# The order of a copy and a matmul product in the value pair of a fused attention and SwiGLU kernel

## The chip, the cores and the metric

The kernel runs on one core of a Trainium2 chip. The core has a matrix engine (TensorE, PE in the profile, with its weight loads as PEld), VectorE (DVE), ScalarE (ACT), GpSimd (POOL) and SyncE (SP, which here only issues transfers). Each engine works through its own instructions in order and waits on semaphores for the others. The metric is the device time of one execution in microseconds.

## What is computed

The reference is an attention with keys and values projected from 1024 to 64 rows, followed by a gated feed-forward block (cut, with the softmax and the joining of the heads written as calls):

```python
# batch 8, heads 8, seq 1024, head_dim 64, k_proj 64; d_model 512, d_ff 1536
k_proj = np.einsum('ks,bhsd->bhkd', E, k)
v_proj = np.einsum('ks,bhsd->bhkd', F, v)
scores = scale * np.matmul(q, k_proj.transpose(0, 1, 3, 2))
attn = softmax(scores)
x = heads_together(np.matmul(attn, v_proj))     # 8192 x 512
g = x @ w_gate
silu = g * (1.0 / (1.0 + np.exp(-g)))
val = x @ w_val
out = silu * val @ w_out                        # 8192 x 512, float32
```

Most of the arithmetic is in the three products of the feed-forward block. The change is in the second, `val = x @ w_val`.

## The kernel before, in words

**Tiling.** The 8192 rows are cut into 16 chunks c of 512 rows (two per batch). For a chunk the attention leaves `xT`: 128 partitions by 4 blocks of the contraction by 512 rows, in bfloat16. The 1536 columns of the two first weights are 12 feature blocks f of 128. The main loop runs over t = 12c + f. For each t it records the gate block (`f_g`: four matmuls of 512 columns at L530 into the PSUM tile `gps`, then ScalarE's activation, L547 or L554), one slot of attention work for a later batch, the value block (`f_v`: four matmuls at L530 into the PSUM tile `vps`, then VectorE's multiplication with the activated gate into `hT`, L648), and the "late" work: sums and products of the output stage for the chunk before (`f_m`, matmuls at L732 into `yps`, with VectorE's addition at L761) and sums that prepare products to come. The order is written out by hand: each engine executes in the order in which the code records its instructions, and the framework adds the semaphore waits that the data need.

**The value pair.** In the 13 chunks c = 2 to 14 the feature blocks 10 and 11 are not computed as two value blocks but as a pair, by a scheme of seven products in place of eight (as in Strassen's method), with the contraction, the features and the rows each cut in two. A product m (`p_mm`, L602) is two matmuls of 256 columns. Products 3 and 4 multiply plain weight blocks by differences of row blocks (`xsa`, `xsb`, made at L593 by GpSimd when c is even, by VectorE when c is odd, several blocks earlier); product 1 multiplies a sum of weights by a sum of rows.

`f_v_pair` is recorded in two parts. The first, at f = 10, takes a PSUM tile `xp` (named `vps`, two halves of 256 columns, one bank), puts product 3 in its first half and product 4 in its second, and forms on VectorE, in the SBUF tile `vt`: a copy of product 3 (L618), plus product 4 (L620). It takes a second PSUM tile `zp` (also `vps`) for product 1 and forms the next partial sum (L623). The second part, at f = 11, adds products 5 and 2 onto the halves of `xp`, subtracts these from both partial sums (L630), multiplies the two inner quarters into `hT` (L631), adds products 6 and 7 onto `zp`, and finishes the outer quarters (L636, L638). Of the tiles named `vps` there are two in turn: feature block 8 and `xp` use one, feature block 9 and `zp` the other. So the first matmul into `zp` must follow the multiplication that read feature block 9.

**Around it.** Between the two parts TensorE has the late work of f = 10 (12 matmuls at L732) and the gate block of f = 11. On VectorE the instructions around the copy are, in even chunks before the last pair (c = 14), the multiplication L648 of block 9, a sum and a reciprocal of the softmax (L402, L403), the copy, L620, L623, L761; in odd chunks L648 and a difference (L593) come before the copy, in c = 14 L648 alone. GpSimd meanwhile multiplies softmax rows (L417), adds up a check sum (`zsum`, L433) and forms sums for the output stage (L715). A second path of the program (`general`), taken only when the check sum is too large, makes no pairs.

Of the kernel before, what the change touches and what calls it, by code (L numbers as in the profile page):

```python
# [44 lines left out]
def kernel(  # L45
# [115 lines left out]
    def bank(where, shape, dt, name):  # L161
        if where == "a" and ring["wide"]:
            where = "aaz"[ring["n"] % 3]
            ring["n"] += 1
        pool, tag = banks[where]
        return pool.tile(shape, dt, name=name, tag=tag)
# [428 lines left out]
    def p_mm(c, m, ps, start=False):  # L595

        x = xT[divmod(c, CH)]
        f = [slice(i * P, (i + 1) * P) for i in PAIR]
        w = {3: wv[:, 0:2, f[0]], 4: wv[:, 2:4, f[1]]}[m] if m in (3, 4) else sums["w", m]
        xs = {2: x[:, 0:2, 0:HT], 5: x[:, 2:4, HT:CW]}[m] if m in (2, 5) else sums["x", m]  # L600
        for kt in range(2):
            nc.tensor.matmul(  # L602
                out=ps,
                lhsT=w[:, kt],
                rhs=xs[:, kt],
                start=(start and kt == 0),
                stop=(kt == 1),
                skip_group_check=True,
            )

    def f_v_pair(c, f):

        tensor_tensor = nc.vector.tensor_tensor
        if f == PAIR[0]:
            xp = gp["x"] = bank("v", [P, 2, HT], FP32, "vps")
            t = gp["t"] = fw.tile([P, 2, HT], FP32, name="vt", tag="s1", bufs=1)
            p_mm(c, 3, xp[:, 0], start=True)
            nc.vector.tensor_copy(out=t[:, 0], in_=xp[:, 0])  # L618
            p_mm(c, 4, xp[:, 1])
            tensor_tensor(out=t[:, 0], in0=t[:, 0], in1=xp[:, 1], op=ALU.add)  # L620
            zp = gp["z"] = bank("v", [P, 2, HT], FP32, "vps")
            p_mm(c, 1, zp[:, 0], start=True)
            tensor_tensor(out=t[:, 1], in0=t[:, 0], in1=zp[:, 0], op=ALU.add)  # L623
            return
        th, xp, zp, t = (gp.pop(i) for i in "pxzt")
        th = th[:].rearrange("p i t -> p (i t)")
        h = hT[c][:, PAIR[0] : PAIR[1] + 1, :].rearrange("p i t -> p (i t)")
        p_mm(c, 5, xp[:, 0])
        p_mm(c, 2, xp[:, 1])
        tensor_tensor(out=t[:], in0=t[:], in1=xp[:], op=ALU.subtract)  # L630
        tensor_tensor(  # L631
            out=h[:, HT : 3 * HT], in0=th[:, HT : 3 * HT], in1=xp[:].rearrange("p i t -> p (i t)"), op=ALU.mult
        )
        p_mm(c, 6, zp[:, 1])
        p_mm(c, 7, zp[:, 0])
        tensor_tensor(out=t[:], in0=t[:], in1=zp[:], op=ALU.add)  # L636
        h, th = (a.rearrange("p (i t) -> p i t", i=4)[:, 0::3] for a in (h, th))
        tensor_tensor(out=h, in0=th, in1=t[:], op=ALU.mult)  # L638

    def f_v(c, f, i=None):  # L640
        if paired(c, f):
            return f_v_pair(c, f)
        ps = f_mm(c, f, 1, i)
        g, th = gp.pop(0)
        if f == 0:
            hT[c] = h_pool.tile([P, NFT, CW], BF16, name="hT", tag="hT")
        if g is None:
            nc.vector.tensor_tensor(out=hT[c][:, f, :], in0=th[:], in1=ps[:], op=ALU.mult)  # L648
            return
        s1 = fw.tile([P, CW], FP32, name="s1", tag="s1", bufs=1)  # L650
        nc.vector.scalar_tensor_tensor(
            out=s1[:], in0=th[:], scalar=1.0, in1=g[:], op0=ALU.add, op1=ALU.mult
        )
        nc.vector.scalar_tensor_tensor(
            out=hT[c][:, f, :], in0=s1[:], scalar=0.5, in1=ps[:], op0=ALU.mult, op1=ALU.mult
        )
# [258 lines left out]
    with tc.manual_schedule():  # L915
# [175 lines left out]
        for t in range(NIT):  # L1091
            c, f = divmod(t, NFT)
# [42 lines left out]
```

## Time and profile before

| What | Value |
|---|---|
| Median of 3 runs | 555.32 us (555.25 to 555.66) |
| The profiled execution | 555.38 us |
| Its span in the profile | 553.8 us |
| VectorE busy | 369.4 us, 67% |
| GpSimd busy | 356.3 us, 64% |
| ScalarE busy | 262.0 us, 47% |
| L530 into `gps` / into `vps` | 772 / 672 matmuls, 196.6 / 170.9 us |
| L618 copy, L620, L623 | 13 each; medians 425, 422 and 422 ns |
| L602 | 182 matmuls and as many weight loads; matmul medians 272 to 273 ns |

The span runs from the first to the last instruction of the program; the execution takes a little longer. A matmul's duration includes the time in which its result drains, which overlaps the next matmul: the sum of durations is larger than the busy time, and the pace of TensorE is read from the distance of starts. "Idle before" in a timeline is the time since the engine's last modelled end, and the name behind the arrow is the instruction whose semaphore came last before the start.

### The profile page before, as it was taken

Reading aid. Unit: us, or ns where it says so; the run is one execution under the profiler, and the core shown is the slowest. Engines: PE = TensorE matmul, PEld = TensorE weight load, DVE = VectorE, ACT = ScalarE, POOL = GpSimd, SP = SyncE. Lnnn points to the kernel's source line nnn. Section 1 sums busy time; section 2 is a strip of 40 time slices with the busy share of each in tenths; the row PEclk is TensorE's granted clock in tenths of the full one; section 3 lists DMA queues with packets and bytes.
Section 4 is the critical chain, followed back from the end, with each engine's and each line's share of the span. In section 5 each row is a group of like instructions: output and inputs, shape, how many; then the busy total and the mean of one; then the engine's idle time right before and its main releaser. Section 6 shows DMA issues by size and latency. Waiting matters only on the chain.

```text
span 553.8 us, 9681 instructions
## 1 busy us (share of the span) xinstructions
PE 537.7 (97%) x3636; PEld 320.8 (58%) x3636; DVE 369.4 (67%) x640; ACT 262.0 (47%) x441; POOL 356.3 (64%) x456
## 2 busy tenths in 40 slices
PE   7999999999999999999999999999999999999996
PEld 4654445565556655566565665566555565556565
DVE  3787886677567765668576585666855777555553
ACT  3565454663446624546436454455444653443331
POOL 6862498577567765586665866668656766464262
PEclk9999999999999999999999999999999999999999
DMA  9999979829921798109941199304991122110113
GB/s 199 190 196 189 176 145 181 162 76 162 192 67 40 132 206 156 39 2 179 195 121 39 24 187 198 88 38 60 203 195 39 40 77 76 40 39 0 39 39 118
DMA packets 112227, 62.92 MB, mean 114 GB/s; under 512 B 65968, under 2 KB 103856, under 8 KB 112176
## 3 DMA queue, kind: packets, MB, share of 16 engines
q0 software_dynamic: 43952, 29.49, 37.7%
q1 hardware_dynamic: 67392, 31.46, 25.0%
q10 hardware_dynamic: 832, 1.31, 0.7%
q8 instruction: 29, 0.48, 0.4%
q14 instruction: 22, 0.18, 0.1%
HBM read 60.29 MB, written 16.78 MB: 139 GB/s over the span
## 4 chain that ended last, share of the span: by engine, by line
PE 87%; ACT 4%; POOL 3%; DMA 2%; DVE 2%; issue 2%; ACTq 0%; POOLq 0%; DVEq 0%
PE gps L530 27%; PE vps L530 24%; PE yps L732 23%; PE vps L602 4%; DMA wv<-in_moe_w_val_dram 2%; PE sc L372 2%; PE kvp L181 2%; PE yps L666 2%; ACT L554 1%; PE pv L476 1%; ACT ee L380 1%; POOL AAd L417 1%; DVE hT L648 1%; POOL hs L715 1%; ACT th L554 1%
## 5 line engine op out<-in xcount | busy, mean ns | idle before, releaser
L530 PE MATMUL gps<-xT,wg 128*128 128x512 bf16 (+1 forms) x772 | 196.6, 377 | 0.0
L530 PE MATMUL vps<-xT,wv 128*128 128x512 bf16 (+1 forms) x672 | 170.9, 377 | 0.7 <-DMA wv<-in_moe_w_val_dram 0.7
L715 POOL TENSOR_TENSOR hs<-hT 128x256 bf16<-128x256 bf16 x180 | 120.7, 695 | 53.6 <-DVE hT L648 30.6
L554 ACT ACTIVATE th<-gps 128x512 f32<-128x512 f32 x130 | 77.6, 597 | 151.3 <-PE gps L530 142.1
L648 DVE TENSOR_TENSOR hT<-th,vps 128x512 bf16<-128x512 f32 x130 | 88.6, 681 | 80.4 <-PE vps L530 66.5
L530 PEld LDWEIGHTS <-wv 128*128 128x128 bf16 x672 | 64.4, 98 | 77.6 <-issue 3.8
L732 PEld LDWEIGHTS <-hs 128*128 128x128 bf16 x900 | 88.0, 98 | 29.1 <-issue 0.6
L530 PEld LDWEIGHTS <-wg 128*128 128x128 bf16 x776 | 74.0, 98 | 51.6 <-issue 0.5
L417 POOL TENSOR_TENSOR AAd<-ee,zr 128x512 bf16<-128x512 f32 x56 | 58.3, 1041 | 35.9 <-DVE zr L403 28.9
L762 POOL TENSOR_TENSOR tt<-tt,ysb 128x512 f32<-128x512 f32 x28 | 35.6, 1272 | 66.2 <-DVE tt L761 66.2
L732 PE MATMUL yps<-ws,hs 128*128 128x256 bf16 x540 | 68.6, 273 | 0.2 <-DVE ysb L801 0.2
L715 DVE TENSOR_TENSOR hs<-hT 128x1536 bf16<-128x1536 bf16 (+1 forms) x49 | 60.1, 1231 | 0.1
L402 DVE TENSOR_REDUCE zr<-ee 128x8 f32<-128x512 f32 x64 | 43.4, 678 | 18.7 <-ACT ee L380 18.7
L732 PE MATMUL yps<-ws,hT 128*128 128x256 bf16 x360 | 48.8, 273 | 0.0
L732 PE MATMUL yps<-wo,hs 128*128 128x256 bf16 x360 | 48.6, 273 | 0.1
L732 PEld LDWEIGHTS <-hT 128*128 128x128 bf16 x360 | 35.2, 98 | 16.1
L593 POOL TENSOR_TENSOR xsa<-xT 128x512 bf16<-128x512 bf16 (+1 forms) x21 | 40.4, 1950 | 0.0
L380 ACT ACTIVATE ee<-sc 128x512 f32<-128x512 f32 x64 | 35.7, 607 | 4.3 <-PE sc L372 2.9
L751 POOL TENSOR_TENSOR tt<-xs 128x256 f32<-128x256 f32 x30 | 22.7, 758 | 22.3 <-ACT xs L749 22.3
L547 ACT ACTIVATE thp<-gps 128x512 f32<-128x512 f32 x26 | 15.5, 598 | 31.7 <-PE gps L530 31.7
L756 ACT COPY ysb<-yps 128x512 f32<-128x512 f32 x30 | 17.6, 585 | 27.3 <-PE yps L732 27.3
L749 ACT COPY xs<-yps 128x512 f32<-128x512 f32 x30 | 17.7, 590 | 25.1 <-PE yps L732 25.0
(131 smaller groups left out, 577.7 us busy)
## 6 DMA issues: line engine op xcount, KB each, us to landing
out_dram<-ysb SPq DMA_DIRECT2D x27, 512.0 KB, 3.0
qb<-in_q_dram POOLq DMA_DIRECT2D x14, 512.0 KB, 17.1
kb<-in_k_dram POOLq DMA_DIRECT2D x7, 1024.0 KB, 11.8
vb<-in_v_dram POOLq DMA_DIRECT2D x7, 1024.0 KB, 14.1
wo<-in_moe_w_out_dram POOLq DMA_DIRECT2D x2, 768.0 KB, 21.9
out_dram<-ysb SPq DMA_DIRECT2D x6, 256.0 KB, 2.4
kraw<-in_k_dram ACTq DMA_DIRECT2D x2, 512.0 KB, 4.9
qb<-in_q_dram POOLq DMA_DIRECT2D x4, 256.0 KB, 7.9
```

The lines of the kernel that those rows point to most:

```text
L380: nc.scalar.activation(out=e[:].rearrange("p h j k -> p (h j k)"), in_=ps[:].rearrange("p a k -> p (a k)"), func=AF.Exp, scale=scale,)
L402: nc.vector.reduce_sum(out=z, in_=e[:], axis=AX.X)
L417: eng.tensor_tensor(out=a.rearrange("p j h k -> p h j k"), in0=ee.pop((b, u))[:], in1=r.unsqueeze(3).to_broadcast([P, 4, 2, KP]), op=ALU.mult,
L530: nc.tensor.matmul(out=ps[:, ts], lhsT=(wg, wv)[w][:, kt, f * P : (f + 1) * P], rhs=x[:, kt, ts], start=(kt == 0), stop=(kt == NKT - 1),)
L554: nc.scalar.activation(out=th[:], in_=ps[:], func=AF.Silu)
L593: eng.tensor_tensor(out=sums["x", m], in0=i0, in1=i1, op=op)
L602: nc.tensor.matmul(out=ps, lhsT=w[:, kt], rhs=xs[:, kt], start=(start and kt == 0), stop=(kt == 1), skip_group_check=True,)
L648: nc.vector.tensor_tensor(out=hT[c][:, f, :], in0=th[:], in1=ps[:], op=ALU.mult)
L715: eng.tensor_tensor(out=hs[c, m][:, fs, :], in0=quarter(hT[c], *a)[:, fs], in1=quarter(hT[c], *b)[:, fs], op=op,)
L732: nc.tensor.matmul(out=ps, lhsT=lhsT, rhs=ws[m][:, f, :] if rhs is None else rhs, start=(start and f == 0), stop=(f == HF - 1), skip_group ...
L751: nc.gpsimd.tensor_tensor(out=t[:, 0], in0=xs[:, 0], in1=xs[:, 1], op=ALU.add)
L762: nc.gpsimd.tensor_tensor(out=t[:], in0=t[:], in1=yo[c, p][:, 1:3], op=ALU.subtract)
```

## The change

In the first part of the value pair two statements change places: the code records product 4's matmuls ahead of VectorE's copy of product 3.

```diff
             p_mm(c, 3, xp[:, 0], start=True)
+            p_mm(c, 4, xp[:, 1])
             nc.vector.tensor_copy(out=t[:, 0], in_=xp[:, 0])
-            p_mm(c, 4, xp[:, 1])
             tensor_tensor(out=t[:, 0], in0=t[:, 0], in1=xp[:, 1], op=ALU.add)
             zp = gp["z"] = bank("v", [P, 2, HT], FP32, "vps")
             p_mm(c, 1, zp[:, 0], start=True)
```

The copy is L618 before and L619 after. As the two are on different engines, the order of the instructions on each engine stays as it was; what differs is which instruction waits for which. The values computed are the same.

## The prediction

> **What bounds the kernel now.** I read the page first, then who TensorE waited for, then the timeline around the edited lines.
>
> ```profile
> span 553.8 us, 9681 instructions
> PE 537.7 (97%) x3636; PEld 320.8 (58%) x3636; DVE 369.4 (67%) x640; ACT 262.0 (47%) x441; POOL 356.3 (64%) x456
> PEclk9999999999999999999999999999999999999999
> ```
>
> TensorE (PE) is busy 97% of the span at an undiminished clock, and no other engine passes 67%. So the time is the sum of what TensorE issues and of the moments in which it can't issue. The next view lists those moments: what waited, for whom, microseconds in total, times, longest. Of its eight rows these are the three largest.
>
> ```profile
> PE vps L602 <- DVE vt L618: 4.3, 8, 0.6
> PE vps L602 <- POOL zsum L433: 2.9, 5, 0.6
> PE warm L954 <- DVE zeros L932: 1.4, 1, 1.4
> ```
>
> L602 is the matmul of the value pair. It was held 8 + 5 = 13 times, once in each of the 13 paired chunks; together 7.2 us. The other six rows (1.4 and five under 1 us) are single events of the start and the tail. So in the steady part TensorE has one kind of stall, and it is in the edited lines. In an even chunk (c = 4) it looks like this; columns are start, duration, engine, line, what, and the idle time with its releaser.
>
> ```profile
> 176.25 0.65 DVE L648 TENSOR_TENSOR hT<-th,vps 128x512 bf16<-128x512 f32 x1
> 177.12 0.38 PE L602 MATMUL vps<-xsa,wv 128*128 128x256 bf16 x2
> 177.53 0.20 DVE L403 RECIPROCAL zr<-zr 128x8 f32<-128x8 f32 x1
> 177.65 0.37 DVE L618 COPY vt<-vps 128x256 f32<-128x256 f32 x1
> 177.83 0.22 POOL L433 TENSOR_TENSOR zsum<-zsum,zr 128x16 f32<-128x16 f32 x1
> 178.08 0.39 PE L602 MATMUL vps<-xsb,wv 128*128 128x256 bf16 x2 [0.58 <-POOL zsum L433]
> 178.31 0.38 PE L602 MATMUL vps<-xsa,xsb 128*128 128x256 bf16 x2
> 178.51 0.42 DVE L620 TENSOR_TENSOR vt<-vt,vps 128x256 f32<-128x256 f32 x1 [0.49 <-PE vps L602]
> 178.53 1.47 PE L732 MATMUL yps<-ws,hs 128*128 128x256 bf16 x12
> 179.03 0.42 DVE L623 TENSOR_TENSOR vt<-vt,vps 128x256 f32<-128x256 f32 x1
> 180.11 0.42 DVE L761 TENSOR_TENSOR tt<-tt,yps 128x256 f32<-128x256 f32 x1 [0.65 <-PE yps L732]
> 180.70 0.60 PE L602 MATMUL vps<-xT,xsb 128*128 128x256 bf16 x4
> 181.14 0.27 PE L602 MATMUL vps<-xsa,xsb 128*128 128x256 bf16 x1
> ```
>
> Product 3 is issued at 177.12, VectorE copies its result from 177.65 to 178.02, and product 4 starts at 178.08, 0.06 us behind the copy's end. Product 4 writes the other half of the PSUM tile that the copy reads, and the listing of the program's instructions has its first weight load wait for the copy. In an odd chunk (c = 3) TensorE shows the same step:
>
> ```profile
> 143.12 0.39 PE L602 MATMUL vps<-xsa,wv 128*128 128x256 bf16 x2
> 144.03 0.38 PE L602 MATMUL vps<-xsb,wv 128*128 128x256 bf16 x2 [0.52 <-DVE vt L618]
> ```
>
> **The stall's price.** One 256-column matmul is issued every (1.47 - 0.27) / 11 = 0.109 us: the row of 12 at 178.53 takes 1.47, and one alone lasts 0.27. Two take 0.22. So c = 4 loses 178.08 - 177.12 - 0.22 = 0.74 us, and c = 3 loses 144.03 - 143.12 - 0.22 = 0.69. The waits view shows less (0.58 and 0.52) because it counts from the modelled end of the last matmul, which comes 0.273 - 0.109 = 0.164 us after the next could have been issued. Over all: 7.2 + 13 x 0.164 = 9.3 us.
>
> **The change part by part.** Nothing is added and every engine keeps its order; the listings of both programs differ in waits alone.
>
> 1. *Removed: product 4's wait for the copy.* It keeps a wait for its input difference: on GpSimd in even chunks (L593 at 165.30 for 1.16 us in c = 4, over 10 us early) and on VectorE in odd ones (the view of L593 has the first of these at 141.8 for 0.42, in c = 3, 0.9 us ahead of product 3). Neither holds it. So product 4 is issued right behind product 3: -9.3 us.
>
> 2. *Added: a wait in front of product 1.* It writes the pair's second tile, whose last reader is the multiplication of feature block 9 (L648). Earlier that was covered by the wait for the copy. In c = 4 that L648 ends at 176.90, before product 3 starts, while product 1 would now be issued at 177.12 + 4 x 0.109 = 177.56. It is met 0.66 us early and I take its cost as 0. From below: a met wait may be free, and the spacing around the old wait may even tighten by 0.01 a chunk, 0.1 in all. From above: if the hand-over can't overlap, it costs the 0.06 us seen from copy end to product 4 and a 0.10 us weight load, 0.16 x 13 = 2.0 us. No row shows a met wait at this place. The nearest are products 5 and 2 at 180.70: product 5 and, from 181.14, product 6 carry met waits for L620 and L623 in the listing, and the four matmuls between take 0.44, 0.110 each. So I take 0.
>
> 3. *Moved: the copy.* It now waits for product 4. In c = 4 that product would be issued at 177.34 and 177.45, and done at 177.45 + 0.27 = 177.72; VectorE comes free of L403 at 177.73. With the 0.04 us that the copy took to start after its product in c = 3 (143.12 + 0.39 = 143.51, start 143.55), the copy runs from 177.76 at the odd chunks' 0.43 us to 178.19. In even chunks it is thus not delayed by more than 0.1 us, because VectorE was behind anyway; in odd ones it starts 0.22 us later.
>
> 4. *Queued behind the copy on VectorE:* L620, L623, then L761 and the rest. L620 no longer waits for TensorE. With the 0.10 us between L620's end (178.93) and L623's start, L620 runs 178.29 to 178.71 and L623 178.81 to 179.23. What is late next? L761 is released by TensorE, and its 180.11 becomes 180.11 - 0.74 = 179.37: VectorE is free 0.14 us before. Product 5 (180.70, now 179.96) overwrites what L620 reads: 1.25 us to spare. So the copy's 0.43 us is hidden by what TensorE issues between products 4 and 5: product 1, the 12 matmuls of L732 and the four of the next gate block. If that cover were gone, product 5 would wait up to 0.43 + 0.10 us a chunk, 6.9 us in all.
>
> The Trainium skill, page "VectorE: DVE Perf Modes", section "The DRAIN you can't avoid", speaks against item 4: after each VectorE operation it puts a flush of its duration less 266 ns, 0.16 us here, where the row has 0.10. By that page the estimate has L623 end 0.11 us later, still 0.03 before L761 is released, so the sum would be the same by both.
>
> Sum: -9.3 + 0 + 0. The profiled execution took 555.38 us, 1.55 more than its span; the median of the runs is 555.32. So the span goes to 544.5 and the time to 555.3 - 9.3 = **546.0 us**. TensorE's stages are all released by TensorE's own earlier work, so that a shift early on stays: where VectorE waited for TensorE (L620, L761 above) it waits still.
>
> **The rivals.**
>
> *A. In five even chunks GpSimd is the releaser.* The waits view says so: POOL zsum L433, five times. That sum runs 177.83 to 178.05, just before product 4. If it were so, five chunks would keep 0.74 us each, 3.7 us: 549.7 us. Against it: product 4's GpSimd wait in the listing is for L593 of the block differences, long done; the copy ends within 0.03 us of the sum by accident of this stage. 4%.
>
> *B. The wait only moves.* If product 1 had to wait for the copy itself, it would start at 178.19 + 0.06 = 178.25 instead of 178.31 in even chunks (0.06 won), and in odd ones at 144.24 instead of 144.25. That is 6 x 0.06 + 7 x 0.01 = 0.4 us: 554.9 us. For it: the copy still stands between the products in VectorE's queue and TensorE's wait is counted in VectorE's operations. Against: the count in the listing is that of L648, and product 1 writes another tile. 4%.
>
> *C. Slower: VectorE's chain becomes late at product 5.* One mechanism: L620 now stands behind a later copy, and product 5 waits for it. It costs from the point where L620 ends 1.25 us later than I have it, and it eats the whole gain at 1.25 + 0.72 = 1.97 us. At 2.1 us late the loss is 13 x 0.13 = 1.7: 557.0 us. For it: in even chunks VectorE has no idle time between L648 and the copy. Against: it would take four more operations of 0.42 + 0.10 us in that queue, and the order has none. 3%.
>
> **How the numbers follow.** My forecast has 88%, A 4%, B 4%, C 3%, and 1% is left for what I don't see. Range of the forecast: from 545.5 (the 0.1 of item 2 and the runs' spread of 0.4) to 548.0 (the 2.0 of item 2). As it holds 88%, it need not reach to A. A measurement here can tell about 0.2%, 1.1 us. Faster: forecast and A, 92%. Within: B and the rest, 5%. Slower: C, 3%.
>
> **What would show it.** Right: the waits view has no row of L602 for L618 or L433; products 3, 4 and 1 stand 0.22 us apart; TensorE is busy 537.7 - 13 x 0.164 = 535.6 us (the tails now overlap) of a span near 544.5, 98%. Item 3: the copy starts about 0.04 us after product 4 or right behind L403. Item 4: L620 has no idle time for TensorE before it, L761 still has some. Wrong: a row L602 for L648 or L619 (B), a gap ahead of the four matmuls of L602 near 180 (C), or a PEclk below 9, which would be a cause outside this list.

## The result and the profile after

| | before | after |
|---|---|---|
| Median of 6 runs | 555.40 us (555.05 to 555.66) | 546.95 us (546.61 to 547.50) |
| The profiled execution | 555.38 us | 547.50 us |
| Its span | 553.8 us | 545.8 us |

The ratio is 0.9849, with a 95% interval of 0.9836 to 0.9861: 8.45 us less, where 9.3 were forecast. The head of the page after:

```profile
span 545.8 us, 9668 instructions
PE 535.5 (98%) x3636; PEld 321.5 (59%) x3636; DVE 369.6 (68%) x640; ACT 262.2 (48%) x441; POOL 356.2 (65%) x456
PEclk9999999999999999999999999999999999999999
```

The clock is the same, and TensorE's busy time fell by 2.2 us. Of this, 430.69 - 429.12 = 1.57 lie behind the first product 3 (c = 2): the 13 matmul tails of 0.164, which now overlap the next matmul, less the 0.09 at seven places that is told below. The other 0.6 lie in front of it, where the two programs are the same. The 13 instructions that are gone are waits: L620 had two and has one. The view of what TensorE waited for, four largest of nine rows:

```profile
PE warm L954 <- DVE zeros L932: 1.4, 1, 1.4
PE vps L530 <- DMA wv<-in_moe_w_val_dram: 0.9, 1, 0.9
PE sc L372 <- DVE BD L169: 0.7, 1, 0.7
PE efp L942 <- DMA Eraw<-in_E_dram: 0.7, 1, 0.7
```

L602 is gone from it, for L618 and for L433. What is left are single events of the start and the tail. The timeline of the even chunk c = 4:

```profile
175.66 0.65 DVE L648 TENSOR_TENSOR hT<-th,vps 128x512 bf16<-128x512 f32 x1
...
176.52 0.38 PE L602 MATMUL vps<-xsa,wv 128*128 128x256 bf16 x2
...
176.74 0.38 PE L602 MATMUL vps<-xsb,wv 128*128 128x256 bf16 x2
...
176.94 0.20 DVE L403 RECIPROCAL zr<-zr 128x8 f32<-128x8 f32 x1
176.96 0.38 PE L602 MATMUL vps<-xsa,xsb 128*128 128x256 bf16 x2
...
177.16 0.42 DVE L619 COPY vt<-vps 128x256 f32<-128x256 f32 x1
177.18 1.47 PE L732 MATMUL yps<-ws,hs 128*128 128x256 bf16 x12
177.24 0.22 POOL L433 TENSOR_TENSOR zsum<-zsum,zr 128x16 f32<-128x16 f32 x1
...
177.62 0.42 DVE L620 TENSOR_TENSOR vt<-vt,vps 128x256 f32<-128x256 f32 x1
178.14 0.42 DVE L623 TENSOR_TENSOR vt<-vt,vps 128x256 f32<-128x256 f32 x1
...
178.76 0.42 DVE L761 TENSOR_TENSOR tt<-tt,yps 128x256 f32<-128x256 f32 x1 [0.19 <-POOL hs L715]
...
179.35 0.60 PE L602 MATMUL vps<-xT,xsb 128*128 128x256 bf16 x4
```

Products 3, 4 and 1 and the first of L732 stand 0.22 us apart, the pace of two matmuls. Product 1's new wait, for L648, was met 0.65 us before it started. GpSimd's sum starts 0.5 us after product 4, so product 4 does not need it. VectorE's chain ends at 178.56, 0.2 ahead of L761. L761 stands 1.58 us behind the first of L732, as it did before (178.53 to 180.11): it is still TensorE that it waits for, although the row names GpSimd. In c = 14 the same 0.19 is put down to L732.

In the odd chunk c = 3 one distance is off. ScalarE's row is the four casts out of the attention's PSUM tiles (L485), which it makes in a row.

```profile
143.23 2.05 ACT L485 CAST xT<-pv 128x512 bf16<-128x512 f32 x4
143.34 0.38 PE L602 MATMUL vps<-xsb,wv 128*128 128x256 bf16 x2
...
143.56 0.38 PE L602 MATMUL vps<-xsa,xsb 128*128 128x256 bf16 x2
...
143.87 1.47 PE L732 MATMUL yps<-ws,hs 128*128 128x256 bf16 x12
```

From product 1 to L732 it is 0.31 us, not 0.22. The first matmul of L732 takes the PSUM bank that the first of these casts empties; a cast's median is 0.598 us, so that cast ends at 143.23 + 0.60 = 143.83, and the matmul starts 0.04 behind it. In the same chunk before, the casts stood where they stand now:

```profile
143.24 2.05 ACT L485 CAST xT<-pv 128x512 bf16<-128x512 f32 x4
...
144.46 1.47 PE L732 MATMUL yps<-ws,hs 128*128 128x256 bf16 x12
```

L732 came 144.46 - 143.84 = 0.62 us behind the cast. The change would bring it 0.69 us nearer, and it needs the 0.04 behind the cast's end. By these rounded rows 0.11 us has to be given back (0.69 + 0.04 - 0.62); the distance shows 0.09 (0.31 - 0.22). It is so in each of the six odd chunks, and in c = 2, where the distance is the same 0.31: 0.6 us in all.

### The profile page after: what moved, and what is told of

Same layout as the page of the kernel before. It is cut to its first block, busy times and chain, and to the rows that moved or that the text cites. A ratio compares the mean times of both kernels' runs of the same rounds, so it can differ in the third digit from the quotient of the medians.

```text
span 545.8 us, 9668 instructions
## 1 busy us (share of the span) xinstructions
PE 535.5 (98%) x3636; PEld 321.5 (59%) x3636; DVE 369.6 (68%) x640; ACT 262.2 (48%) x441; POOL 356.2 (65%) x456
## 4 chain that ended last, share of the span: by engine, by line
PE 88%; DMA 8%; POOL 2%; issue 0%; ACT 0%; DVE 0%; POOLq 0%; DVEq 0%; ACTq 0%
PE gps L530 28%; PE yps L732 25%; PE vps L530 24%; PE vps L602 4%; DMA qTd<-qb 3%; PE sc L372 2%; DMA qb<-in_q_dram 2%; PE kvp L181 2%; DMA Fraw<-in_F_dram 1%; PE pv L476 1%; PE yps L666 1%; DMA wv<-in_moe_w_val_dram 1%; POOL wv L144 0%; POOL AA L417 0%; POOL wg L144 0%
## 5 line engine op out<-in xcount | busy, mean ns | idle before, releaser
L554 ACT ACTIVATE th<-gps 128x512 f32<-128x512 f32 x130 | 77.6, 597 | 151.2 <-PE gps L530 140.2
L648 DVE TENSOR_TENSOR hT<-th,vps 128x512 bf16<-128x512 f32 x130 | 88.6, 681 | 81.0 <-PE vps L530 67.1
L732 PEld LDWEIGHTS <-hs 128*128 128x128 bf16 x900 | 88.0, 98 | 29.7 <-issue 0.6
L732 PE MATMUL yps<-ws,hs 128*128 128x256 bf16 x540 | 68.6, 272 | 0.2 <-DVE ysb L801 0.2
L732 PE MATMUL yps<-ws,hT 128*128 128x256 bf16 x360 | 48.8, 273 | 0.0
L732 PE MATMUL yps<-wo,hs 128*128 128x256 bf16 x360 | 48.6, 273 | 0.1
L732 PEld LDWEIGHTS <-hT 128*128 128x128 bf16 x360 | 35.2, 98 | 16.0
L551 ACT ACTIVATE th<-gps 128x512 f32<-128x512 f32 x35 | 20.9, 598 | 16.7 <-PE gps L530 15.4
```

Of the source, the lines that this page charges most:

```text
L554: nc.scalar.activation(out=th[:], in_=ps[:], func=AF.Silu)
L732: nc.tensor.matmul(out=ps, lhsT=lhsT, rhs=ws[m][:, f, :] if rhs is None else rhs, start=(start and f == 0), stop=(f == HF - 1), skip_group ...
```

## The experiments

All times are medians, beside the kernel before on the same chip (555.47 us in the first four, 555.52 in the others); a ratio is to that kernel, with its 95% interval in brackets. Each diff is against the changed kernel.

**The exchange in the even chunks alone.**

```diff
-            p_mm(c, 4, xp[:, 1])
+            if c % 2 == 0:
+                p_mm(c, 4, xp[:, 1])
             nc.vector.tensor_copy(out=t[:, 0], in_=xp[:, 0])
+            if c % 2 != 0:
+                p_mm(c, 4, xp[:, 1])
```

> The exchange is made in the seven even chunks alone (c = 2, 4, ... 14); the odd ones keep the copy between the products. My theory: product 4's wait in even chunks is for the copy, although the waits view named GpSimd's zsum in five of them. The stalls read from the timeline of before are 0.80 (c = 2), 5 x 0.74 and 0.68, less the 0.09 that c = 2 gives back at L732 in the profile of after: 5.1 us off 555.4, so 550.3 us (549.9 to 550.8), and no row of L602 for L433. Rival A (GpSimd is the releaser in five even chunks): only c = 2 and c = 14 gain, 1.4 us, so 554.0 us, and the five waits for L433 stay.

550.06 us, ratio 0.990 [0.9885, 0.9915]. The largest row of TensorE's waits:

```profile
PE vps L602 <- DVE vt L620: 3.1, 6, 0.5
```

L620 is the copy's line in this kernel. The six odd stalls are left, and none is named for GpSimd. A gain of 5.4 us fits the stalls read for seven even chunks (5.1), not the 1.4 of rival A. What the waits view named in those five was an event that came just before the start, not the one waited for.

**The exchange in the odd chunks alone**: the same edit with the parity turned.

> The exchange is made in the six odd chunks alone. My theory: the stalls of 0.68 go, and 0.09 comes back in each as the distance from product 1 to the first matmul of L732 (0.20 in place of 0.11), where that matmul now waits for ScalarE's cast of a PSUM bank (L485). 6 x 0.59 = 3.5 us off 555.4: 551.9 us (551.4 to 552.3); with even_only the two gains sum to that of the whole change. Rival (nothing is given back inside the chunks, and what the change lacks against the forecast lies in the start of the program alone): 6 x 0.68 = 4.1 us, 551.3 us.

551.79 us, ratio 0.9933 [0.9919, 0.9946]: 3.7 us. This lies between 3.5 and 4.1, too near to both to decide by the medians. TensorE's timeline of c = 3 decides:

```profile
143.34 0.38 PE L602 MATMUL vps<-xsa,xsb 128*128 128x256 bf16 x2
143.65 1.47 PE L735 MATMUL yps<-ws,hs 128*128 128x256 bf16 x12
```

It is 0.31 again (L735 is L732 here). The two halves sum to 5.4 + 3.7 = 9.1 us, beside 8.45 and 8.7 us in two measurements of the whole change; the runs of one kernel spread over 0.3 to 1.2 us, so this is a sum within what can be told. The table of starts, further on, allows a closer sum.

**Product 1 between the copy and product 4.**

```diff
             p_mm(c, 3, xp[:, 0], start=True)
-            p_mm(c, 4, xp[:, 1])
             nc.vector.tensor_copy(out=t[:, 0], in_=xp[:, 0])
-            tensor_tensor(out=t[:, 0], in0=t[:, 0], in1=xp[:, 1], op=ALU.add)
             zp = gp["z"] = bank("v", [P, 2, HT], FP32, "vps")
             p_mm(c, 1, zp[:, 0], start=True)
+            p_mm(c, 4, xp[:, 1])
+            tensor_tensor(out=t[:, 0], in0=t[:, 0], in1=xp[:, 1], op=ALU.add)
```

> The copy stays right behind product 3, but product 1 (which writes the other PSUM tile) is issued before product 4 (which writes the tile that the copy reads). My theory: product 4 alone waits for the copy and starts at the same distance from product 3 as before, while product 1's 0.22 us is now spent inside the wait: 13 x 0.22 = 2.8 us off 555.4, 552.6 us (552.0 to 553.2), and the waits view keeps 13 rows of L602 for the copy, each 0.22 shorter. Rival (any product behind the copy waits for it, whatever tile it writes): 555.4 us. Second rival (it is enough that the next product is of another tile; the stall goes whole): 547 us.

552.73 us, ratio 0.9949 [0.9936, 0.9963]: 2.7 us. The timeline of c = 4:

```profile
176.51 0.38 PE L602 MATMUL vps<-xsa,wv 128*128 128x256 bf16 x2
...
176.73 0.38 PE L602 MATMUL vps<-xsa,xsb 128*128 128x256 bf16 x2
...
177.05 0.37 DVE L618 COPY vt<-vps 128x256 f32<-128x256 f32 x1
...
177.48 0.39 PE L602 MATMUL vps<-xsb,wv 128*128 128x256 bf16 x2 [0.36 <-POOL zsum L433]
```

Product 1, of the other tile, goes at TensorE's own pace. Product 4 starts 0.97 us behind product 3, as before (0.96), and 0.06 behind the copy's end. The waits view again puts five of the 13 waits down to GpSimd's sum, where I expected all at the copy; the two rows together fell from 7.2 to 4.3 us, 0.22 a chunk. So the stall was the wait for the copy out of product 4's own tile, and it can be filled with whatever writes elsewhere. Both rivals fall.

**Another bank for the attention's fourth product.** The change, and:

```diff
-        put(s0 + 44, u_PVt, b, 0, (0, 1), ("aa", "yz"))
+        put(s0 + 44, u_PVt, b, 0, (0, 1), ("aa", "yg"))
```

> The change as it is, and in the odd chunks the attention's fourth product takes a PSUM bank of the gate ring in place of the bank that the first matmul of L732 writes behind product 1. My theory: in the odd chunks that matmul waited for ScalarE's cast out of that bank; the distance from product 1's second matmul to it falls from 0.20 to 0.11 us in six chunks, 0.54 us in all: 546.4 us (546.0 to 546.8) beside 546.95 for the change alone; c = 2 keeps its 0.20. Rival (the 0.09 is a cost of the weight load or of VectorE's reading beside TensorE, not of that bank): the distance stays 0.20 and the time 546.95.

546.01 us (545.93 to 546.53), ratio 0.9831 [0.9817, 0.9844]. The timeline of c = 3:

```profile
142.41 2.05 ACT L485 CAST xT<-pv 128x512 bf16<-128x512 f32 x4
...
142.74 0.38 PE L602 MATMUL vps<-xsa,xsb 128*128 128x256 bf16 x2
...
142.96 1.47 PE L732 MATMUL yps<-ws,hs 128*128 128x256 bf16 x12
```

The distance is 0.22, with the casts as late against TensorE as they were. So the 0.09 was the wait for that bank. In c = 2, which this edit doesn't touch, the distance stays 0.31, as expected. From product 3 of c = 2 to the end of the span it is 544.5 - 110.97 = 433.5 us, beside 545.8 - 111.78 = 434.0 for the change alone: the 0.5 us expected. This version has the lowest median of all; of the 0.94 us by which it lies below 546.95, only these 0.5 are shown to come from the bank.

**Two kernels again, for their starts.**

> The kernel before, unchanged, for a second profile of its start. My theory: what the change lacks against the forecast beyond the 0.6 us given back at L732 is the start of the program, which differs from run to run with its transfers: product 3 of c = 2 began at 111.06 us in the profile of before and at 111.79 in that of after, though both programs are the same up to there. It should begin anywhere between 110.8 and 111.9 here, with the time within 555.0 to 555.8. Rival (the change itself makes the start later): here within 0.1 of 111.06 again.

> The changed kernel, unchanged, for a second profile of its start. My theory: product 3 of c = 2 begins between 110.8 and 111.9 us and not at 111.79 again; the distance from there to the end of the span is 434.0 within 0.1 as in the first profile; time 546.6 to 547.2. Rival (the change itself makes the start later): within 0.1 of 111.79 again.

The same program gave 555.33 and 546.79 us (ratio to before 0.9842 [0.9828, 0.9855] for the latter). The start of product 3 of c = 2, up to which all of these are the same program:

| profile | product 3 of c = 2, us | span - that |
|---|---|---|
| before | 111.06 | 442.7 |
| before, again | 110.98 | 442.8 |
| after | 111.78 | 434.0 |
| after, again | 111.35 | 434.1 |
| after, other bank | 110.97 | 433.5 |
| after, two more copies | 111.07 | 434.2 |
| after, five more copies | 110.89 | 445.1 |
| exchange in even chunks | 110.96 | 437.5 |
| exchange in odd chunks | 110.83 | 439.3 |
| product 1 between | 110.90 | 439.8 |

The two profiles of the changed kernel differ by 0.43, and they are the latest of the ten. Two profiles of before agree within 0.1, which by itself is what the rival said; that five other versions with the exchange, three of them with it in all chunks, start at 110.83 to 111.07 speaks against it. Behind the start the change is worth 442.7 - 434.0 = 8.7 us. The halves, reckoned so before rounding, are worth 5.23 and 3.55, in sum 8.78. Here the odd half fits 3.5 (0.09 given back in each chunk) and not the rival's 4.1.

**Two, then five more copies on VectorE.** In the changed kernel, behind the copy:

```diff
+            for _ in range(2):
+                nc.vector.tensor_copy(out=t[:, 1], in_=xp[:, 0])
```

They write a half of `vt` that is overwritten before it is read.

> The changed kernel with two more copies of product 3 on VectorE behind the first, into the half of vt that L623 overwrites later: they add about 0.45 to 0.53 us each to the chain between product 4 and product 5. My theory: the cover between products 4 and 5 is 1.2 us a chunk (1.25 in the forecast), so that 0.9 to 1.06 us of it is hidden: 546.9 to 547.8 us, no row of L602 for VectorE in the waits view above 0.3 us in all. Rival C's reading (VectorE's chain stands close behind TensorE there): product 5 waits in each chunk, 13 x 0.5 to 1.0 us: 553 us or more.

546.86 us, ratio 0.9844 [0.9828, 0.9859]: 26 more VectorE instructions cost nothing that can be measured. In c = 3 the addition starts 1.13 us behind the first copy in place of 0.46, so the two moved it by 0.67, less than I expected and about half of the cover.

> The same with five more copies: 2.25 to 2.65 us more on VectorE's chain. My theory: the cover of 1.2 us is used up, and product 5 waits for L620, or product 6 for L623, by 1.0 to 1.4 us in each of the 13 chunks: 560 to 566 us. If the time stays below 550, the cover is larger than I read it; if it is above 575, it was not there at all.

557.53 us, ratio 1.004 [1.0025, 1.0056]: below the range that I gave. The view of TensorE's waits has one large row, and the timeline of c = 3 shows it (L622 is L620 here):

```profile
PE vps L602 <- DVE vt L622: 7.4, 13, 0.6
```

```profile
144.02 0.42 DVE L619 COPY vt<-vps 128x256 f32<-128x256 f32 x1 [1.52 <-PE vps L602]
...
144.37 2.25 DVE L621 COPY vt<-vps 128x256 f32<-128x256 f32 x5
...
145.44 1.03 PE L530 MATMUL gps<-xT,wg 128*128 128x512 bf16 x4
...
146.53 0.41 DVE L622 TENSOR_TENSOR vt<-vt,vps 128x256 f32<-128x256 f32 x1
147.00 0.60 PE L602 MATMUL vps<-xT,xsb 128*128 128x256 bf16 x4 [0.53 <-DVE vt L622]
...
147.05 0.42 DVE L625 TENSOR_TENSOR vt<-vt,vps 128x256 f32<-128x256 f32 x1
...
147.52 0.60 PE L602 MATMUL vps<-xsa,xsb 128*128 128x256 bf16 x4
```

Five copies moved the addition from 0.46 behind the first copy's start (143.76 and 144.22 in after) to 2.51: 2.05 us, 0.41 each and not 0.45 or more. Product 5 stalls for 0.53 + 0.164 = 0.7 us, so 2.05 - 0.7 = 1.35 was hidden. In c = 4 product 5 stands 3.61 us behind product 3 in place of 2.83, so 2.05 - 0.78 = 1.27 was hidden there. Over all the waits come to 7.4 + 13 x 0.164 = 9.5 of the 10.7 us. Most of the rest is product 6: it writes the tile that L625 (L623 in the other kernels) reads, starts 0.05 behind L625's end (147.47), and stands 0.52 us behind product 5, where it is 0.44 in after (179.35 and 179.79 in c = 4): 13 x 0.08 = 1.0. The place and the kind of the wait are as expected; I had over-sized what a copy adds.

## Why the prediction was right, and where it was short

**Item 1, product 4's wait (9.3 us): right.** Products 3 and 4 now stand 0.22 us apart, and the even and odd halves of the change gave 5.4 and 3.7 us where the stalls read from the timeline were 5.2 and 4.1. The sign that I gave, a busy time of 535.6 us, was met (535.5) partly by luck: behind the first product 3 the busy time fell by 1.57 and not by 2.1, and the start of the program, which the change doesn't touch, supplied the rest.

**Item 2, product 1's new wait (0, at most 2.0): right at its lower end.** It is met 0.65 us early (forecast 0.66), and the distance to product 1 is 0.22.

**Item 3, the copy's new place: right.** It starts at 177.16, 0.04 behind product 4's end (177.12) and just after VectorE comes free of L403 (177.14), 0.64 us behind product 3's start as forecast (177.76 - 177.12). In c = 14, where VectorE is idle before it, it is 0.64 too.

**Item 4, the chain behind it: right in VectorE, and short on ScalarE.** VectorE's cover of 1.25 us between products 4 and 5 was shown to be there: two more copies are hidden, five are not, and the hidden part is 1.27 in c = 4, for which it was forecast, and 1.35 in c = 3. The step that was off is the sum, "-9.3 + 0 + 0". Under "what is late next" I followed VectorE's queue and product 5, and counted the 12 matmuls of L732 as cover without asking what releases them. Their first waits for ScalarE's cast, which stays where it was while TensorE comes 0.69 us earlier; 0.62 us of distance was there. The term that I put at 0 measured 7 x 0.09 = 0.6 us, and a bank that isn't shared takes it to 0 in six of the seven chunks. "TensorE's stages are all released by TensorE's own earlier work" was too broad: the casts too follow TensorE's matmuls, but ones that stand ahead of the stall, and these don't move with it. The same sentence of the prediction has L620 go on waiting for TensorE, against its own item 4; the profile has L620 right behind the copy, as item 4 said.

With it the forecast is 546.0 + 0.6 = 546.6 us, beside medians of 546.95 and 546.79. The rest, 0.2 to 0.35 us, is no more than the runs of one kernel differ by (546.45 to 547.50). Behind the start nothing is left of it: 9.3 - 0.6 is the 8.7 measured there. What makes a start early or late was not tried; the first profile of after has a wait for a transfer (`PE sc L372 <- DMA qTd<-qb: 0.5, 1, 0.5`) that the first profile of before has not, but the second profile of before, which starts early, has one of 0.4 too. That 546.95 lies inside the range is in part luck: the range reached up to 548.0 for a cost in front of product 1, which was not paid, and not for ScalarE's cast, which was.

**The rivals.** A fell by the even half (550.06, not 554.0). B fell by the profile: no row of L602 is left. (By item 3's own figures B's odd chunks have 143.55 + 0.22 + 0.43 + 0.06 = 144.26, not 144.24, which moves B by 0.1 us and changes nothing.) C's place is real: with five more copies product 5 waits for the addition and the kernel is slower than before, by 0.4%. Its condition, 1.97 us later than forecast, lies close to the 2.05 at which this was measured.

## What to carry to other kernels

When a result is copied out of a PSUM tile whose other half is still to be written, record the writes first: the wait then lies with the reader, which had time here, and not with TensorE, which had none. How much time the reader has is to be read first; here it was 1.3 us, and five more copies used it up. When a stall is removed, list every engine whose work was released ahead of the stall and is needed behind it; each must have been early by more than the stall, or it sets what is left. A name in a waits view is the last event before the start: before believing it, look for a stage in which that event comes at another time, or change the kernel in half of the stages.

## What the runs showed of the hardware

An instruction of VectorE that needs the one before it starts sooner than I took: L620 at 177.62, 0.04 us behind the copy's end (177.16 + 0.42), while L623, which waits for TensorE as well, starts 0.10 behind L620's (178.04). Where product 1 came earlier and L623 waited for VectorE alone, in the kernel with product 1 between (L622 is L620 here), it too started 0.04 behind:

```profile
177.91 0.42 DVE L622 TENSOR_TENSOR vt<-vt,vps 128x256 f32<-128x256 f32 x1 [0.49 <-PE vps L602]
178.37 0.42 DVE L623 TENSOR_TENSOR vt<-vt,vps 128x256 f32<-128x256 f32 x1
```

So the 0.10 that I used as the gap between dependent instructions is 0.04 for the dependence and 0.06 to 0.07 for a second wait (0.034 and 0.104 us before rounding, in 13 chunks of each kernel). The flush of 0.16 us that the Trainium skill gives ("VectorE: DVE Perf Modes", "The DRAIN you can't avoid") is not seen as a gap between these rows, and the measurement decides here. The same passage lets an operation that isn't held start earlier, and the first extra copy, which needs nothing of the one before, starts at 144.37, 0.07 before that one's end.

While VectorE reads one bank (L619, from 177.16), TensorE writes another at full pace: the 12 matmuls of L732 take 1.47 us in that stretch, 0.109 each, which is the pace of products 3 and 4 (0.22 for two), when VectorE reads no PSUM.
